# Staging all attention scores in two on-chip tiles, with partition-aligned copies in place of a trip through device memory

## The chip, the core and the metric

The kernel runs on one NeuronCore of a Trainium2 chip. Its engines work side by side and meet at semaphores: TensorE (PE; its weight loads are shown as PEld), VectorE (DVE), ScalarE (ACT), GpSimd (POOL) and SyncE (SP), whose queue issues nearly all DMAs. On-chip memory (SBUF) and the matmul accumulators (PSUM) both have 128 partitions; device memory (DRAM) is reached by DMA alone. The metric is device time in microseconds of one execution, median of several.

## What is computed

Attention with "talking heads" (a 12 by 12 mix of the heads ahead of the softmax and another behind it), followed by two dense layers of the form in, activation, out:

```python
# attention: batch 2, heads 12, positions 448, head size 64
scores = scale * q @ k.T                       # per head
scores = einsum("bhij,hg->bgij", scores, w_pre)
attn   = exp(scores - max) / (sum + 1e-9)      # over j
attn   = einsum("bgij,gh->bhij", attn, w_post)
x      = (attn @ v) as 896 rows of 768
# layer 1: h = x @ w_in (768 to 2048); g = h * clip(h + 3, 0, 6) / 6;  x = g @ w_out
# layer 2: h = x @ w_in2; g = P(h) / (Q(h) + 1e-6);                    out = g @ w_out2
```

The weights and data are float32 in value; the weights of the dense layers arrive as 64-bit words and are turned into float32 on the chip.

## The kernel before, in words

**Chunks and pairs.** The 448 query rows of a batch are cut into four chunks of 120, 120, 120 and 88 rows, eight chunks in all. A chunk is worked in groups of 10 query rows, two groups being a pair: six pairs in a chunk of 120, five in one of 88, 46 in all. The main loop has one step for each pair m, from 0 to 45.

**A step.** `premix(m)` (L265) multiplies the scores of the pair by the head-mixing weights, into two PSUM tiles M of 448 columns. The rows of a group, 10 positions times 12 heads, lie in partitions. DVE takes the row maxima (L272), ACT the exponentials (L274), `norm` gets the reciprocals (L281, L282) and POOL the scaled weights `wr` (L284). Two steps later `postmix` (L308) mixes the heads again into PSUM tile A, and `at_evac` (L316, ACT) copies it to `at`. In between, by fixed tables of step numbers, stand `scores` for a later chunk (L244: two head pairs, four matmul tiles, copied out by DVE at L249, two in the same step and two "held" for the next) and `av_unit` (L331: the product with v of an earlier chunk, X, evacuated by ACT at L343 and DVE at L344 into the high and low parts `XH` and `XL` of the layers' input).

**How scores get from "query row in partition" to "position and head in partition".** Copying out of PSUM leaves a tile with one query row per partition. `premix` needs a group's 120 (position, head) rows in partitions.
- Chunks 0 and 1 are staged whole in `stage` and `stage1`. `spread_pair` (L226) then copies a pair straight inside SBUF, as two DMAs of 210 KB (10 source partitions, 120 target partitions), to partitions 0 to 119. There `premix` multiplies with all 120 rows at once, with weights `wp0` that hold zeros for the other half.
- Chunks 2 to 7 are staged two heads at a time in a ring of four. `put_heads` (L216) sends each piece to a tile of device memory that has 60 rows and 4 zero rows per half group, and `get_pair` (L231) fetches a pair three steps ahead. There `premix` multiplies two sets of 60 rows, at partitions 0 and 64.

`stage1` occupies the memory that later becomes `XL`.

**What sets the order.** Up to L668 the order on every engine is the order of the program text; each engine works through its own queue in that order. DMAs go out on SP's queue in program order, with eight semaphores in turn, so that a ninth waits for the first. `SCORES`, `VALUES`, `LQ`, `LV` and `LK` say in which steps scores, v products and loads of q, v and k stand. The first weights of layer 1 are loaded from step 32 (`LOADS`) and converted by ACT (L399), DVE (L401, L403, L407) and POOL (L423, L424) from step 35 (`PIECES`). `FILL` puts parts of the first products of layer 1 (L351 to L353, `h`) into steps 39, 41 and 42. Behind the loop stand the last two `postmix`, the rest of those products and the last chunk's v products.

Of the kernel before, what the change touches and what calls it, by code (L numbers as in the profile page):

```python
# [48 lines left out]
def fused_kernel(  # L49
# [101 lines left out]
    nc.scalar.dma_start(out=wrep0, in_=w_pre[None, :, :].to_broadcast([GR, H, H]))  # L151
    zeros = front.tile([2 * MG * (64 - HP), S], F32, name="zeros")

    def put_pads(t):
        nc.sync.dma_start(out=t.rearrange("g (a p) s -> (g a) p s", a=2)[:, HP:], in_=zeros)

    def load_w(i):
        for a in range(0, 128, 64):
            nc.sync.dma_start(out=wrep[a : a + HP, i, :], in_=(w_pre, w_post)[i][None, :, :].to_broadcast([HR, H, H]))

    load_w(1)
# [762 lines left out]
```

## Time and profile before

| | us |
|---|---|
| median of 3 runs | 675.83 (673.94 to 678.23) |
| the profiled execution | 675.95 |
| its span, first to last instruction | 674.0 |
| first `premix` starts | 14.73 |
| last step's `premix` starts | 195.03 |
| first product of layer 1 over the second token part starts | 211.93 |

Nearly all of the kernel before 212 us is attention, all of it after that the two dense layers. A span is read from its engine's rows: start, duration, engine, line, operation, and in square brackets the idle time of the engine just before it with what ended it. "x8" merges eight instructions of one kind. A float32 matmul appears as two instructions.

### The profile page before, as it was taken

Reading aid. Unit: us, or ns where it says so; the run is one execution under the profiler, and the core shown is the slowest. Engines: PE = TensorE matmul, PEld = TensorE weight load, DVE = VectorE, ACT = ScalarE, POOL = GpSimd, SP = SyncE. Lnnn points to the kernel's source line nnn. Section 1 sums busy time; section 2 is a strip of 40 time slices with the busy share of each in tenths; the row PEclk is TensorE's granted clock in tenths of the full one; section 3 lists DMA queues with packets and bytes.
Section 4 is the critical chain, followed back from the end, with each engine's and each line's share of the span. In section 5 each row is a group of like instructions: output and inputs, shape, how many; then the busy total and the mean of one; then the engine's idle time right before and its main releaser. Section 6 shows DMA issues by size and latency. Waiting matters only on the chain.

```text
span 674.0 us, 16112 instructions
## 1 busy us (share of the span) xinstructions
PE 653.7 (97%) x6682; PEld 540.4 (80%) x6682; DVE 513.2 (76%) x879; ACT 379.0 (56%) x682; POOL 33.9 (5%) x76
## 2 busy tenths in 40 slices
PE   8998999898899999999999999999999999999997
PEld 3455556555668888988888888889999999999997
DVE  5756667676564999999866565279998999989991
ACT  4655666665664555555423323158575766779851
POOL 1110101011421000000000000000000000000000
PEclk9998999998999999999999999999999999999999
DMA  6778878897643567666542323437657665746512
GB/s 231 244 222 292 302 237 275 264 317 241 201 126 98 164 209 220 200 212 197 176 158 88 125 80 117 187 120 248 223 189 253 200 245 180 245 163 222 192 54 94
DMA packets 77503, 131.61 MB, mean 195 GB/s; under 512 B 6662, under 2 KB 57958, under 8 KB 77430
## 3 DMA queue, kind: packets, MB, share of 16 engines
q1 hardware_dynamic: 77012, 130.20, 58.8%
q8 instruction: 53, 0.87, 0.5%
q10 hardware_dynamic: 418, 0.37, 0.2%
q14 instruction: 20, 0.16, 0.1%
HBM read 90.99 MB, written 34.41 MB: 186 GB/s over the span
## 4 chain that ended last, share of the span: by engine, by line
PE 89%; DMA 3%; issue 2%; DVE 2%; ACT 2%; SPq 1%; POOL 1%; ACTq 0%; POOLq 0%; DVEq 0%
PE h L351 11%; PE h L352 11%; PE h L353 11%; PE A L308 7%; PE y L353 6%; PE y L351 6%; PE acc L351 6%; PE acc L352 6%; PE acc L353 6%; PE y L352 6%; PE M L265 6%; PE sc L244 5%; PE X L331 5%; SPq L226 1%; DMA keys<-in_k_dram 1%
## 5 line engine op out<-in xcount | busy, mean ns | idle before, releaser
L352 PE MATMUL h<-xl,wh 128*128 128x512 f32 (+1 forms) x384 | 140.1, 365 | 1.1 <-issue 1.1
L351 PE MATMUL h<-xh,wh 128*128 128x512 f32 (+1 forms) x384 | 140.6, 366 | 0.4 <-DVE g L516 0.4
L353 PE MATMUL h<-xh,wl 128*128 128x512 f32 (+1 forms) x384 | 139.1, 362 | 0.0
L272 DVE TENSOR_REDUCE st<-M 128x1 f32<-128x448 f32 x92 | 54.1, 620 | 41.8 <-PE M L265 41.0
L274 ACT ACTIVATE e<-M,st 128x448 f32<-128x448 f32 x92 | 57.6, 631 | 40.5 <-DVE st L272 40.5
L351 PEld LDWEIGHTS h<-xh,wh 128*128 128x128 f32 x384 | 72.1, 188 | 8.9 <-issue 0.8
L352 PEld LDWEIGHTS h<-xl,wh 128*128 128x128 f32 x384 | 72.2, 188 | 8.1 <-issue 1.4
L353 PEld LDWEIGHTS h<-xh,wl 128*128 128x128 f32 x384 | 72.1, 188 | 8.1
L426 ACT ACTIVATE wh<-wf 128x768 fp32r<-128x768 f32 (+1 forms) x52 | 42.6, 819 | 63.1 <-PE y L352 50.7
L427 DVE TENSOR_TENSOR wl<-wf,wh 128x768 fp32r<-128x768 f32 (+1 forms) x52 | 48.0, 924 | 36.1 <-ACT wh L426 36.1
L399 ACT ACTIVATE wf<-wraw 128x768 f32<-128x768 f32 (+1 forms) x56 | 49.5, 885 | 41.1 <-DVE wl L427 39.9
L353 PE MATMUL y<-gh,wl 128*128 128x384 f32 x192 | 70.6, 368 | 0.0
L351 PE MATMUL y<-gh,wh 128*128 128x384 f32 x192 | 70.5, 367 | 0.0
L352 PE MATMUL y<-gl,wh 128*128 128x384 f32 x192 | 69.9, 364 | 0.0
L308 PEld LDWEIGHTS A<-wr,e 60*56 60x56 f32 x2944 | 45.2, 130 | 26.7 <-issue 21.9
L316 ACT COPY at<-A 120x960 f32<-120x960 f32 x46 | 45.0, 979 | 33.2 <-PE A L308 33.0
L308 PE MATMUL A<-wr,e 60*56 60x60 f32 x2944 | 52.1, 219 | 6.6 <-issue 4.8
L403 DVE SCALAR_TENSOR_TENSOR wf<-wraw,icst,wf 128x768 int32<-128x768 int32 (+1 forms) x56 | 55.3, 988 | 1.0
L265 PE MATMUL M<-full,wp 60*64 60x448 f32 (+1 forms) x368 | 55.5, 557 | 0.3 <-ACT e L274 0.3
L407 DVE SCALAR_TENSOR_TENSOR wf<-wraw,icst,wf 128x768 int32<-128x768 int32 (+1 forms) x56 | 55.2, 986 | 0.8
L331 PEld LDWEIGHTS X<-at,vraw 120*64 120x64 f32 x768 | 37.3, 137 | 18.2 <-issue 12.5
L244 PE MATMUL sc<-keys,qraw 64*120 64x448 f32 (+1 forms) x192 | 44.3, 569 | 4.0 <-DVE xl L344 1.9
(98 smaller groups left out, 1141.8 us busy)
## 6 DMA issues: line engine op xcount, KB each, us to landing
wraw<-in_moe_w_out_dram SPq DMA_DIRECT2D x28, 768.0 KB
wraw<-in_moe_w_in_dram SPq DMA_DIRECT2D x22, 768.0 KB
full<-scores SPq DMA_DIRECT2D x34, 448.0 KB
scores<-stg SPq DMA_DIRECT2D x24, 420.0 KB
wpre<-in_moe_w_in_dram SPq DMA_DIRECT2D x10, 768.0 KB
w2h<-wh SPq DMA_DIRECT2D x16, 384.0 KB
w2l<-wl SPq DMA_DIRECT2D x16, 384.0 KB
ws<-w2h SPq DMA_DIRECT2D x16, 384.0 KB
```

The source lines that it names most:

```text
L244: nc.tensor.matmul(sc[i][:n, :S], lhsT=qraw[C][o, hp, :n], rhs=keys[b][o, hp], start=True, stop=True)
L265: nc.tensor.matmul(mt[a][64 * c : 64 * c + 64, :S], lhsT=wp[o] if C >= DIRECT else wp0[:, a], rhs=src[o if C >= DIRECT else slice(0, GR * ...
L272: nc.vector.tensor_reduce(out=st[:, a : a + 1], in_=mt[a][:, :S], op=ALU.max, axis=AX.X, negate=True)
L274: nc.scalar.activation(out=e[:, a], in_=mt[a][:, :S], func=AF.Exp, bias=st[:, a : a + 1], accum_out=st[:, 2 + a : 3 + a])
L308: nc.tensor.matmul(av[64 * c : 64 * c + JH, r, jc, :, a * HR : a * HR + HR], lhsT=e[o, a, j : j + JH], rhs=wr[o, a], start=True, stop=True,)
L331: nc.tensor.matmul(X[hh % 2 * D : hh % 2 * D + D, hh % 4 // 2, :n], lhsT=vs[:, jc, :], rhs=at[C][:, jc, hh, :n], start=(jc == 0), stop=(jc ...
L351: nc.tensor.matmul(o, lhsT=wh, rhs=mh, start=first, stop=False)
L352: nc.tensor.matmul(o, lhsT=wh, rhs=ml, start=False, stop=False)
L353: nc.tensor.matmul(o, lhsT=wl, rhs=mh, start=False, stop=last)
L399: nc.scalar.activation(out=w, in_=hw.bitcast(F32), func=AF.Copy, scale=2.0**-112)
L403: nc.vector.scalar_tensor_tensor(out=wi, in0=hw, scalar=icst[:, 0:1], in1=wi, op0=ALU.bitwise_and, op1=ALU.bitwise_or)
L407: nc.vector.scalar_tensor_tensor(out=wi, in0=lw, scalar=icst[:, 1:2], in1=wi, op0=ALU.logical_shift_right, op1=ALU.bitwise_or)
```

## The change

All eight chunks are staged whole, in two tiles used in turn (`stages[C % 2]`). `spread_pair` copies every pair inside SBUF, into partitions 4 to 123 of a ring of five pairs (`first`); partitions 0 to 3 are zeroed once. A group's rows then lie in partitions 4 to 63 and 64 to 123, and `premix` of every pair multiplies two sets (64 and 60 rows). The device-memory tiles, `put_heads`, `get_pair`, their zero rows and `wp0` go; `XL` gets memory of its own. The pair for step m + 4 is copied in step m. A chunk's scores stand nine, seven and five steps ahead of its first pair. The weights' pool opens in step 37, where the front pool is freed; each weight tile is loaded in three DMAs. `FILL` goes, and the products that it placed stand behind the loop.

```diff
+LOW = 64 - HP
 NCH = 4
 MG = CH // GR
 NP = H // 2
-DIRECT = 2
-LEAD = 3
+RING = 5
...
-    scd = {}
-    sct = [dram.tile([MG, 128, S], F32, name=f"scores{i}") for i in range(3)]
-
...
-    wrep = front.tile([128, 2, H], F32, name="wrep")
-    mask0 = front.tile([GR * H, GR], F32, name="mask0")
-    wrep0 = front.tile([GR * H, H], F32, name="wrep0")
+    wrep = front.tile([128, H], F32, name="wrep")
+    mask0 = front.tile([128, 2, HR], F32, name="mask0")
+    wrep0 = front.tile([128, H], F32, name="wrep0")
+    first = att.tile([128, RING, 2, S], F32, tag="first", bufs=1, name="first")
+    stages = [att.tile([CH, H, S], F32, tag=f"stage{i}", bufs=1, name=f"stage{i}") for i in range(2)]
...
     XH = xp.tile([128, KD, NT], F32R, name="xh")
-    place = xp.tile([128, KD, NT], F32, tag="xl", name="stage1")
-    stage1 = place.rearrange("p c t -> p (c t)").rearrange("p (h s) -> p h s", s=S)[:CH]
-
+    XL = xp.tile([128, KD, NT], F32R, name="xl")
...
+    nc.vector.memset(first[:LOW, :2], 0.0)
...
+    nc.gpsimd.memset(wp, 0.0)
+    nc.gpsimd.memset(first[:LOW, 2:], 0.0)
...
-    def put_heads(C, hp, st):
-        n = chunks[C][3]
-        rows = scd[C][:n].rearrange("g (a p) s -> (g a) p s", a=2)[:, :HP]
-        nc.sync.dma_start(
-            out=rows.rearrange("x (i h) s -> x i (h s)", h=H)[:, :, 2 * hp * S : (2 * hp + 2) * S],
-            in_=st[: n * GR].rearrange("p h s -> p (h s)"),
-        )
-
     def spread_pair(m):
         C, g0 = pairs[m]
-        full[m] = spread.tile([128, 2, S], F32, tag="first", bufs=NP, name=f"full{m}")
-        rows = (stage, stage1)[C].rearrange("p h s -> p (h s)").rearrange("(r g) x -> g r x", g=MG)
+        full[m] = first[:, m % RING]
+        G = chunks[C][3]
+        rows = stages[C % 2][: G * GR].rearrange("p h s -> p (h s)").rearrange("(r g) x -> g r x", g=G)
         for c in range(2):
-            nc.sync.dma_start(out=full[m][: GR * H, c, :], in_=rows[g0 + c])
-
-    def get_pair(m):
-        C, g = pairs[m]
-        full[m] = att.tile([128, 2, S], F32, tag="full", bufs=LEAD, name=f"full{m}")
-        nc.sync.dma_start(out=full[m], in_=scd[C][g : g + 2].rearrange("g p s -> p g s"))
-
-
-    def scores(C, hp, tag="sc", st=None):
+            nc.sync.dma_start(out=full[m][LOW : LOW + GR * H, c, :], in_=rows[g0 + c])
+
+    def scores(C, hp, tag="sc"):
         n = chunks[C][3] * GR
         b = chunks[C][0]
-        if hp == 0:
-            scd[C] = sct[C % 3]
         sc = [ps.tile([128, 512], F32, tag=tag, bufs=BUFS[tag], name=f"sc{C}_{2 * hp + i}") for i in range(2)]
-        if st is None:
-            st = front.tile([CH, 2, S], F32, tag="raw", bufs=4, name=f"stg{C}_{hp}")
+        st = stages[C % 2][:, 2 * hp : 2 * hp + 2]
         for i in range(2):
             o = slice(i * D, i * D + D)
...
-        def take(i, copy):
-            copy(out=st[:n, i], in_=sc[i][:n, :S])
-            if i and C > 1:
-                put_heads(C, hp, st)
-
-        return [lambda copy: take(0, copy), lambda copy: take(1, copy)]
+        return [lambda copy, i=i: copy(out=st[:n, i], in_=sc[i][:n, :S]) for i in range(2)]
...
-                o = slice(64 * a, 64 * a + HP)
+                o = slice(64 * a, 64 + a * HP)
                 nc.tensor.matmul(
-                    mt[a][64 * c : 64 * c + 64, :S], lhsT=wp[o] if C >= DIRECT else wp0[:, a],
-                    rhs=src[o if C >= DIRECT else slice(0, GR * H), c, :], start=True, stop=True,
+                    mt[a][64 * c : 64 * c + 64, :S], lhsT=wp[o],
+                    rhs=src[o, c, :], start=True, stop=True,
...
+    def load_third(u, i):
+        u = units[u]
+        if i == 0:
+            raws[u] = (pools["late"].tile([128, KD * 256], I32, tag="wraw", bufs=2, name="wraw"), KD)
+        n = KD // THIRDS
+        o = raws[u][0].rearrange("p (a b) -> p a b", b=256)[:, i * n : i * n + n]
+        nc.sync.dma_start(out=o, in_=w1i[:, i * n : i * n + n, u[1] * 256 : u[1] * 256 + 256])
...
     for m in range(3):
         spread_pair(m)
     load_q(2)
-    for m in range(3, NP):
+    for m in range(3, RING):
         spread_pair(m)
-    for a in range(2):
-        mix_in(wp0[:, a, :HP].rearrange("p (i g) -> p i g", g=H), mask0[:, a * HR : a * HR + HR], wrep0)
+    mix_in(wp[:, :HP].rearrange("p (i g) -> p i g", g=H), mask0[:, 0], wrep0)
...
     NC = len(chunks)
-    SCORES = list(range(1, 36, 2))
-    VALUES = list(range(8, 38, 2)) + [37, 38, 40, 43, 44, 45]
+    SCORES = [begin[C] - i for C in range(2, NC) for i in (9, 7, 5)]
+    VALUES = [8, 10, 12, 15, 17, 19, 21, 23, 25, 27, 29, 31, 33, 35, 37, 38, 40, 42, 43, 44, 45]
     SC = per_step([(0, (1, hp)) for hp in range(FIRST, NP)] + list(zip(
         sorted(2 * SCORES), [(C, hp) for C in range(2, NC) for hp in range(NP)])))
     XS = per_step(list(zip(
         sorted(2 * VALUES), [(C, i) for C in range(NC - 1) for i in range(NP)])))
-    LQ = {3: 3, 10: 4, 15: 5, 21: 6, 27: 7}
-    LV, LK = {4: 2, 6: 3, 8: 4, 9: 5}, {8: 0, 10: 1, 11: 2, 12: 3, 14: 4, 15: 5}
-    FREE = max(SC) + 2
-    LATE, LOADS = 20, {32: 0, 34: 1, 38: 2, 41: 3}
-    PIECES = dict(zip(range(35, 46), (1, 2, 2, 1, 2, 1, 1, 2, 1, 1, 1)))
-    FILL = {39: (0, 3), 41: (0, 3), 42: (1, 3)}
-    early = {}
-
+    LQ = {2: 3, 8: 4, 14: 5, 19: 6, 25: 7}
+    LV, LK = {3: 2, 5: 3, 6: 4, 7: 5}, {9: 0, 10: 1, 11: 2, 12: 3, 13: 4, 15: 5}
+    LV1 = 28
+    FREE = max(SC) + 1
+    PIECES = dict(zip(range(38, 46), (1, 2, 2, 2, 1, 2, 2, 1)))
+    LOADS = {37: ((0, 0), (0, 1), (0, 2)), 38: ((1, 0), (1, 1)), 39: ((1, 2),)}
+    LOADS.update({40: ((2, 0),), 41: ((2, 1), (2, 2)), 43: ((3, 0), (3, 1)), 44: ((3, 2),)})
...
-        if 1 <= m <= NP:
-            spread_pair(m + NP - 1)
...
-        if first[DIRECT] <= m + LEAD < len(pairs):
-            get_pair(m + LEAD)
...
+        if 1 <= m <= len(pairs) - RING:
+            spread_pair(m + RING - 1)
...
         if m == FREE:
             front.release()
-        if m == LATE:
-            spread.release()
             pools["late"] = tc.alloc_tile_pool(name="late", bufs=1, side="right", reuse_waits="tile")
...
-        if m in LOADS:
-            load_units(LOADS[m])
-        if m in FILL:
-            f, n = FILL[m]
-            if f not in early:
-                early[f] = gemm1(f, 0, ps.tile([128, 512], F32, tag="sc", bufs=BUFS["sc"], name=f"h1_{f}_0"))
-            for _ in range(n):
-                next(early[f])
+        for x in LOADS.get(m, ()):
+            load_third(*x)
     m = len(pairs)
...
-    run(early[1])
+    run(gemm1(0, 0, ps.tile([128, 512], F32, tag="sc", bufs=BUFS["sc"], name="h1_0_0")))
     postmix(m - 2)
     at_evac(m - 2, acopy)
-    h120 = gemm1(2, 0, ps.tile([128, 512], F32, tag="sc", bufs=BUFS["sc"], name="h1_2_0"))
+    h110 = gemm1(1, 0, ps.tile([128, 512], F32, tag="sc", bufs=BUFS["sc"], name="h1_1_0"))
     for _ in range(3):
-        next(h120)
+        next(h110)
     postmix(m - 1)
     at_evac(m - 1, acopy)
     pieces(1)
-    run(h120)
+    run(h110)
     for i in range(NP):
         tail_x(2 * i + 1, "sc" if i < 2 else "M")
+    run(gemm1(2, 0, ps.tile([128, 512], F32, tag="sc", bufs=BUFS["sc"], name="h1_2_0")))
...
+    ucur[0] = 4
     load_units(4)
...
         rows = _np.array([[c[1] + row_of(c, g) + i for g in range(c[3])] for i in range(GR)])
-        rows = q[c[0], :, (rows if C < DIRECT else rows.T).ravel()].reshape(c[3] * GR, NP, 2, D)
+        rows = q[c[0], :, rows.ravel()].reshape(c[3] * GR, NP, 2, D)
```

**SP's queue, around the first pair of chunk 2, before** (`full` is a pair's tile, `stg` two heads of staged scores, `scores_110` and `scores_112` tiles in device memory):

```order
L231 DMA full_795<-scores_112 128x2x448
L135 DMA vraw_5_797<-in_v_dram 120x512
L216 DMA scores_110<-stg_2_801 20x5x896
L231 DMA full_861<-scores_112 128x2x448
L125 DMA qraw_863<-in_q_dram 128x720
L131 DMA keys_721<-in_k_dram 128x448
```

**SP's queue, the same place now** (`stage_128` and `stage_127` are the two staging tiles, `first` the ring):

```order
L130 DMA vraw_5_607<-in_v_dram 120x512
L207 DMA first<-stage_128 120x1x448 x2
L120 DMA qraw_670<-in_q_dram 128x720
L207 DMA first<-stage_127 120x1x448 x2
L126 DMA keys_745<-in_k_dram 128x448
```

A step's one put and one get have become two copies inside SBUF, of half the size each.

**ACT, steps 35 to 36 before** (`e` exponentials, `at` copies, `wf` the first conversion of weight tile 0):

```order
L274 ACTIVATE e_2614,st_2613<-M_0_2607,st_2613 128x448
L274 ACTIVATE e_2614,st_2613<-M_1_2608,st_2613 128x448
L316 COPY at_2350<-A 120x2x48x10
L399 ACTIVATE wf<-wraw 128x768
L274 ACTIVATE e_2680,st_2679<-M_0_2673,st_2679 128x448
```

**ACT now, step 38 and the start of 39:**

```order
L241 ACTIVATE e_2707,st_2706<-M_0_2700,st_2706 128x448
L241 ACTIVATE e_2707,st_2706<-M_1_2701,st_2706 128x448
L310 ACTIVATE xh<-X_1_2712 128x2x120
L283 COPY at_2648<-A 120x2x48x10
L376 ACTIVATE wf<-wraw 128x768
L241 ACTIVATE e_2782,st_2781<-M_0_2775,st_2781 128x448
```

The first conversion stood three steps behind the step of its load, and now stands one step behind it, ahead of step 39's exponentials.

**PE, step 39 before, to the start of step 40** (`M` is premix, `A` postmix, `h_0_0` the first product of layer 1):

```order
L265 MATMUL M_0_2900<-full_2685,wp 64x448 x2
L265 MATMUL M_1_2901<-full_2685,wp 64x448 x2
L308 MATMUL A<-wr_2816,e_2755 56x12x5 x32
L351 MATMUL h_0_0_2953<-xh,wh 128x384
L352 MATMUL h_0_0_2953<-xl,wh 128x384
L353 MATMUL h_0_0_2953<-xh,wl 128x384
...
L265 MATMUL M_0_2963<-full_2760,wp 64x448 x2
```

**PE, step 39 and 40 now:**

```order
L232 MATMUL M_0_2775<-first,wp 64x448 x2
L232 MATMUL M_1_2776<-first,wp 64x448 x2
L275 MATMUL A<-wr_2689,e_2626 56x12x5 x32
L232 MATMUL M_0_2829<-first,wp 64x448 x2
L232 MATMUL M_1_2830<-first,wp 64x448 x2
```

Step 39 has lost its nine products of layer 1; all of `h_0_0` now follows the last step's `postmix`.

## Rows read from the trace of the kernel before

**Rows 1.** The page, part 1: busy time, share of the span, instructions

```profile
PE 653.7 (97%) x6682; PEld 540.4 (80%) x6682; DVE 513.2 (76%) x879; ACT 379.0 (56%) x682; POOL 33.9 (5%) x76
```

**Rows 2.** Windows: stretch, length, busy of PE, PEld, DVE, ACT, POOL, clock, DMA, GB/s

```profile
14.73:64.43 49.70, 47.42 (x858) 24.17 (x860) 32.14 (x75) 26.16 (x60) 4.91 (x13) 0.97 0.78 252
64.43:195.03 130.60, 119.59 (x3091) 78.12 (x3081) 86.66 (x207) 83.75 (x186) 22.14 (x39) 0.99 0.79 253
172.00:200.00 28.00, 25.48 (x643) 18.60 (x631) 17.44 (x38) 16.65 (x37) 9.02 (x10) 1.00 0.44 138
```

**Rows 3.** Timeline of PE, step 5, premix over 120 rows

```profile
31.48 1.72 PE L265 MATMUL M<-full,wp 120*64 120x448 f32 x8
33.14 1.77 PE L244 MATMUL sc<-keys,qraw 64*120 64x448 f32 x8
```

**Rows 4.** Timeline of PE, steps 21 to 23, premix over twice 60 rows

```profile
99.32 0.94 PE L265 MATMUL M<-full,wp 60*64 60x448 f32 x8
100.19 1.77 PE L244 MATMUL sc<-keys,qraw 64*120 64x448 f32 x8
...
102.77 0.94 PE L265 MATMUL M<-full,wp 60*64 60x448 f32 x8
...
106.31 0.94 PE L265 MATMUL M<-full,wp 60*64 60x448 f32 x8
```

**Rows 5.** Timeline of DVE, one short step

```profile
22.88 1.35 DVE L272 TENSOR_REDUCE st<-M 128x1 f32<-128x448 f32 x2 [0.30 <-PE M L265]
24.15 1.15 DVE L249 COPY stg<-sc 120x448 f32<-120x448 f32 x2
...
25.53 1.35 DVE L272 TENSOR_REDUCE st<-M 128x1 f32<-128x448 f32 x2
```

**Rows 6.** Timelines of SP, DVE and PE around step 9

```profile
44.58 2.69 SPq L226 DMA_DIRECT2D full<-stage  x2
51.98 0.41 DVE L344 TENSOR_TENSOR xl<-X,xh 128x240 fp32r<-128x240 f32 x1 [5.44 <-DMA scores<-stg]
52.45 1.29 PE L244 MATMUL sc<-keys,qraw 64*100 64x448 f32 x2 [1.95 <-DVE xl L344]
53.67 1.86 PE L308 MATMUL A<-wr,e 60*56 60x60 f32 x64
55.46 2.18 PE L265 MATMUL M<-full,wp 120*64 120x448 f32 x8
```

**Rows 7.** Timeline of SP: one row is so many DMAs issued together

```profile
10.93 4.98 SPq L226 DMA_DIRECT2D full<-stage  x6
```

**Rows 8.** What PE waited for, 64.43 to 195.03: total, times, longest

```profile
PE A L308 <- issue: 4.8, 5, 2.1
PE X L331 <- issue: 2.0, 3, 0.9
PE h L352 <- issue: 1.1, 1, 1.1
PE sc L244 <- DVE st L272: 1.1, 1, 1.1
```

**Rows 9.** Chain of waits: one 768 KB weight load, start and duration

```profile
212.08 4.68 DMA wpre<-in_moe_w_in_dram
```

**Rows 10.** Timeline of DVE: pieces of a weight tile's conversion

```profile
182.94 0.54 DVE L401 TENSOR_SCALAR wf<-wf 128x768 int32<-128x768 int32 x1
186.89 1.00 DVE L403 SCALAR_TENSOR_TENSOR wf<-wraw,icst,wf 128x768 int32<-128x768 int32 x1
```

**Rows 11.** Timeline of PE behind the loop

```profile
202.60 1.07 PE L308 MATMUL A<-wr,e 60*56 60x60 f32 x64 [0.78 <-ACT at L316]
203.60 0.45 PE L351 MATMUL h<-xh,wh 128*128 128x384 f32 x1
...
205.37 1.06 PE L308 MATMUL A<-wr,e 60*56 60x60 f32 x64
...
211.93 0.50 PE L351 MATMUL h<-xh,wh 128*128 128x512 f32 x1
```

More of the change, by code (lines that the diff above doesn't have):

```diff
@@ L123, in load_q @@
         ns = chunks[C][3] * GR
-        t = front.tile([128, NP, CH], F32, tag="qraw", bufs=3, name=f"qraw{C}")
+        t = front.tile([128, NP, CH], F32, tag="qraw", bufs=2, name=f"qraw{C}")
         eng.dma_start(out=t[:, :, :ns], in_=q[C, :, :, :ns])
@@ L150, in fused_kernel @@
     load_q(1)
[L151 to L161, printed above, removed]
-    nc.gpsimd.memset(mask0, 1.0)
-    nc.gpsimd.affine_select(out=mask0, in_=mask0, pattern=[[-H, GR]], compare_op=ALU.is_ge,
-                            fill=0.0, base=0, channel_multiplier=1)
-    nc.gpsimd.affine_select(out=mask0, in_=mask0, pattern=[[H, GR]], compare_op=ALU.is_ge,
-                            fill=0.0, base=H - 1, channel_multiplier=-1)
-    nc.gpsimd.memset(wp0, 0.0)
-    nc.gpsimd.memset(zeros, 0.0)
-    put_pads(sct[2])
+    nc.scalar.dma_start(out=wrep0[LOW : LOW + GR * H], in_=w_pre[None, :, :].to_broadcast([GR, H, H]))
+    for a in range(0, 128, 64):
+        nc.sync.dma_start(out=wrep[a : a + HP], in_=w_post[None, :, :].to_broadcast([HR, H, H]))
+    nc.gpsimd.memset(mask0, 1.0)
+    nc.gpsimd.affine_select(out=mask0, in_=mask0, pattern=[[-HP, 2], [-H, HR]], compare_op=ALU.is_ge,
+                            fill=0.0, base=-LOW, channel_multiplier=1)
+    nc.gpsimd.affine_select(out=mask0, in_=mask0, pattern=[[HP, 2], [H, HR]], compare_op=ALU.is_ge,
+                            fill=0.0, base=H - 1 + LOW, channel_multiplier=-1)
+    nc.gpsimd.tensor_tensor(out=mask0[:, 0], in0=mask0[:, 0], in1=mask0[:, 1], op=ALU.add)
+    nc.gpsimd.memset(wp, 0.0)
+    nc.gpsimd.memset(first[:LOW, 2:], 0.0)
     for hp in range(2):
@@ L451, in advance @@
         split_units(i + 1)
-    stage = att.tile([CH, H, S], F32, tag="at", bufs=2, name="stage")
     manual = tc.manual_schedule()
@@ L460, in fused_kernel @@
     for hp in range(NP):
-        ev = scores(0, hp, "sc" if hp % 3 else "M", stage[:, 2 * hp : 2 * hp + 2])
+        ev = scores(0, hp, "sc" if hp % 3 else "M")
         ev[0](acopy)
         ev[1](vcopy)
-    def place1(hp):
-        return stage1[:, 2 * hp : 2 * hp + 2]
     for m in range(3):
@@ L521, in fused_kernel @@
     LAG = 2
-    first = [m for m, (C, g) in enumerate(pairs) if g == 0] + [len(pairs)]
+    begin = [m for m, (C, g) in enumerate(pairs) if g == 0] + [len(pairs)]
     def per_step(items):
@@ L571, in fused_kernel @@
             load_v(0, LV[m])
-        if 27 <= m < 27 + NP:
-            load_v(1, m - 27)
+        if LV1 <= m < LV1 + NP:
+            load_v(1, m - LV1)
         if m in LK:
@@ L577, in fused_kernel @@
         for C, hp in SC.get(m, ()):
-            sc += scores(C, hp, st=place1(hp) if C == 1 else None)
+            sc += scores(C, hp)
         for C, i in XS.get(m, ()):
```

19 lines of the change are left out of this document (5 added, 14 removed).

## The prediction

> **What bounds the kernel now.** I read the page first, then the windows by stage, then the timelines of PE, DVE and SP in the attention, and last what PE waited for. The page makes PE the busiest engine by far [rows 1]. That share hides two things: the attention consists of short steps with waits between them, and behind it PE is dense, with the change touching nothing there but the weights that arrive first. So I cost the stretch from the first premix (14.73) to the first product over the second token part (211.93), 197.2 us, and let the rest shift with it. The profiled execution took 675.95 for a span of 674.0, 0.12 above the median; the sum is made against it.
>
> In that stretch a step lasts as long as PE's work in it, when nothing stalls: 3.45 us from premix to premix with scores in it, 3.54 with v products [rows 4]. Steps with neither are held by a loop instead: DVE's maxima, ACT's exponentials, DVE's reciprocal, then the next maxima, 2.65 us from maximum to maximum [rows 5]. The v product and the score copies fit into that loop's gaps.
>
> **What the change removes.**
> - Premix over 120 rows takes 1.66 us to the next operation [rows 3]; over two sets of 60 rows it takes 0.87 [rows 4]. Twelve pairs change, 9.5 us. All else in premix stays; 64 rows instead of 60 stream the same 448 columns, so I take 0.87.
> - The stall of step 9. DVE's first write to `XL` waited 5.44 us for DMAs, since `XL` lies where chunk 1 was staged and the last copy out of it left SP's queue at 47.27 only. PE stood still for 1.95 us, and then ran slow: the clock of the stretch is 0.97 [rows 2], two score instructions took 1.29 instead of 0.43, postmix 1.86 instead of 1.07, premix 2.18 instead of 1.72 [rows 6]. With the gap, 4.0 us go.
> - Device-memory traffic: each of 34 pairs goes through a put and a get of over 400 KB each, and now through one copy of 420 KB. The DMA engines were 0.79 busy [rows 2].
>
> **What it adds.**
> - SP: two issues of 0.83 us each for a pair [rows 7] in place of one put and one get. Under load a pair's issues took 2.69 [rows 6]; both are below a step with its other load beside them, and a pair is copied four steps ahead, so I cost it at nothing. If that cover went, every pair would be late (a rival below). Ahead of the first premix nothing is longer: ten copies instead of twelve, and memsets on engines that stand idle there.
> - Shorter premix makes the short steps PE-idle: steps 1, 2, 4 and 6 have only 0.87 to 1.9 us of PE work and fall back to the loop's 2.65. In step 1, where no postmix stands yet, PE idles for nearly 2 us. By the row after the 1.95 us gap that costs 2.1 more at the lower clock (0.86, 0.79 and 0.46 [rows 6]). Bounds 0 and 2.1; I take 2.1, since the gap is as long.
> - Steps 13 and 14 both carry scores. The second's tiles wait for held copies; the nearest row is a wait of scores for DVE, 1.1 us [rows 8].
> - Weights. The first tile is asked for in step 37 behind two copies, and ACT converts it at the end of step 38, ahead of step 39's exponentials. 768 KB alone took 4.68 us [rows 9]. Behind DVE's last score copies (premix 0.87, maxima 1.35, copies 1.15 [rows 4, 5], 3.4 in all) and the pair's 1.7 us of issue it lands 9.8 us after step 37 starts; ACT gets to it after about 8, a step of 3.54 and the most of another. Bounds: 0, and 4 if the copies hold the load up; I take 1.8.
> - DVE's conversion pieces crowd into steps 39 to 44: 0.55 and 1.0 us apiece [rows 10] on top of the loop. Steps 39 and 41 take 2.65 + 1.55 = 4.2, steps 40 and 42 about 4, step 43 3.6, step 44 about 5, 25 in all. PE may run a premix ahead, so I take 24, against 19.5 without pieces. GpSimd's splits fit before their users.
> - The products taken out of steps 39, 41 and 42 stand behind the loop. There, 9.33 us from postmix 44 on [rows 11] stay, and two whole products (twice 18 matmuls, nine in 1.77 [rows 11]) come on top, 7.1. The wait of 0.78 for ACT goes, hidden by the first of them.
>
> **The sum.** Step 0: 0.87 + 1.70 = 2.6. Four short steps 10.6. Steps 39 to 44: 24. The other 35 at 3.5: 122.5. Tail 9.3 + 7.1 = 16.4. Together 176.1. The same count for the kernel before (premix at 1.66 in steps 0 to 11, nine products in each of steps 39, 41 and 42) is 165.0 for its steps and 11.2 for its tail, 176.2. So the count is a draw: what premix saves, short steps and DVE's pieces take. The gain must come out of the waits, 197.2 − 176.2 = 21 us before. Of these, 4.0 is step 9, 1.1 scores' wait for DVE [rows 8], 0.8 the tail; the other 15 are "issue" waits of PE (4.8 + 2.0 + 1.1 = 7.9 [rows 8]), a second slow stretch behind the longest of them, and small waits.
>
> The issue waits decide the size. They begin with the gets: there is none before 64 us, although DMA was as busy (0.78 and 0.79 [rows 2]). Two of the nine fall where DMA was down to 0.44 [rows 2], each some 5 us behind the issue of a weight load. I read them as PE's instructions held up behind other DMAs. Half the traffic goes, so I take 6.3 of the 15: half of the issue waits, a third of the rest. Bounds 0 and 15, the latter if the early steps, now denser, catch them too.
>
> The Trainium skill, "Runtime: NRT & Kernel Launch", section "Instruction fetch mechanics", says that an engine's instructions come over a DMA queue of its own in blocks of 256, and that crossing a block is mostly hidden. By that rule the 6.3 would be 0 and the time 659; the rows' 7.9 us speak against it.
>
> Waits after: 2.1 + 1.1 + 1.8 + 6.3 = 11.3. Stretch 176.1 + 11.3 = 187.4, 9.8 less than before: 675.95 − 9.8 = 666.2. Three v steps are narrower than I counted, which takes off about 1: **665 us**.
>
> **Rivals.**
> - *The fetch waits vanish* with the traffic: 665 − 6.3 = 659. For it: none in the early steps. Against it: the two at 0.44. Chance 0.18.
> - *They stay or grow*, since they go by instructions and not by traffic: 13 to 15 in place of 6.3, 672. For it: the two at 0.44. Chance 0.18.
> - *Late weights stall ACT for longer.* Tiles 0 and 1 come 2 us later than taken, each stall in front of exponentials idles PE for over 2 us and costs another 2 at the lower clock: 665 + 6 to 7 = 671. Chance 0.08.
> - *Slower: the first pair of every chunk comes late.* Nothing of a chunk can be copied before its last score is staged, which happens in the fourth step ahead of its first pair. From there: 3.4 us to DVE's last copy, 1.7 to 2.7 for SP, and landing, 4.7 for the copy whose issue ended at 47.27 and for which DVE waited until 51.98 [rows 6]. That is 10 to 11 us of four steps' 14. Landing would have to take 12 instead of 4.7; then each of six chunks loses 3.5 us, and the time is 665 + 21 = 686. The decisive point is landing above 8 us. Chance 0.06.
>
> On this last one the Trainium skill, "DMA: Bandwidth & Descriptors", section "Why a DMA increments its semaphore by 16 and not by 1", speaks against the change: the number of DMA engines is the largest up to 16 that divides the outermost sizes of both sides, so 10 for these copies (10 and 120) and 16 for a get. By the row, 210 KB in 0.83 us of issue, two copies fill 1.7 of 3.5 us even so.
>
> **Chances and range.** The forecast itself, 660 to 669, has 0.50. What can be told from no change is 1%, 669.1 and 682.6. Below 669.1: nearly all of the forecast and the first rival, 0.68. Within 1%: the second and third, 0.26. Slower: 0.06. The range 656 to 674 reaches from the first rival to the second with a few us of the unknown costs, and leaves the last out.
>
> **What would show it.** After the change: premix at 0.87 in all steps; no DVE wait for a DMA at step 9; PE idle of 0.8 to 2 us in steps 1, 2, 4 and 6, with a clock below 1 behind step 1; DVE without gaps from step 39 to 44; issue waits of PE in total near half of 7.9; the first product over the second token part near 201. It is wrong if premix waits for DMAs, if the issue waits are not halved, or if ACT's first conversion waits long.

## The result and the profile after

| | before | after |
|---|---|---|
| median of four runs, us | 675.8 (673.94 to 678.23) | 666.53 (665.61 to 669.0) |
| profiled execution, us (span) | 675.95 (674.0) | 665.91 (664.2) |
| stretch, first premix to first product over the second token part | 197.2 | 186.37 |

The ratio is 0.987, with a 95% interval of 0.982 to 0.991: 1.3% faster. On another chip, beside the variants below, the same kernel took 666.96 (664.74 to 667.68) against 677.16, ratio 0.985 (0.981 to 0.989). The forecast was 665, in 656 to 674. The span fell by 9.8 us: the stretch by 10.83, less 0.54 that the first premix started later in this execution and 0.49 behind the stretch.

| part of the stretch, us | before | after |
|---|---|---|
| steps 0 to 11 | 49.70 | 40.11 |
| steps 12 to 38 | 105.83 | 95.86 |
| steps 39 to 44 | 24.77 | 29.70 |
| step 45 | 4.96 | 4.30 |
| tail: from the first product behind the loop | 11.94 | 16.40 |

So 20.2 us were gained, and 9.4 of them went again at the loop's end and behind it, where the products from steps 39, 41 and 42 now stand.

**The early steps.** Timeline of PE in the changed kernel, steps 9 to 11 (columns: start, duration, what, tiles, shapes, number of instructions; in brackets the idle time before it and what ended it):

```profile
44.97 0.94 PE L232 MATMUL M<-first,wp 64*64 64x448 f32 x8
45.84 1.75 PE L216 MATMUL sc<-keys,qraw 64*100 64x448 f32 x8
47.52 1.06 PE L275 MATMUL A<-wr,e 60*56 60x60 f32 x64
48.40 0.94 PE L232 MATMUL M<-first,wp 64*64 64x448 f32 x8
...
51.95 0.94 PE L232 MATMUL M<-first,wp 64*64 64x448 f32 x8
```

This is where [rows 6] stood. Premix takes 0.87 to the next operation, step 9 takes 3.43 us instead of 8.36, and no engine waits for a DMA in these steps.

**The middle.** Windows of the changed kernel: stretch, its length, busy time of PE, PEld, DVE, ACT and POOL, clock, DMA share, GB/s. The first covers steps 0 to 12, one step more than the first of [rows 2]; the last is premix 39 to premix 45:

```profile
15.27:58.92 43.65, 40.35 (x952) 22.26 (x956) 31.52 (x78) 28.19 (x66) 4.64 (x12) 1.00 0.71 226
58.92:144.15 85.23, 83.97 (x2200) 51.06 (x2192) 63.59 (x160) 58.44 (x132) 9.28 (x24) 1.00 0.48 158
64.00:195.00 131.00, 122.36 (x3140) 81.02 (x3140) 90.27 (x210) 84.28 (x186) 20.59 (x38) 0.97 0.45 144
151.24:180.94 29.70, 22.80 (x577) 15.37 (x565) 16.55 (x33) 16.25 (x35) 7.91 (x10) 0.89 0.54 167
```

From 59 to 144 us PE stands still for 1.3 of 85 us. What it waited for up to 202 us (total, times, longest), beside [rows 8]:

```profile
PE M L232 <- ACT e L241: 7.8, 5, 4.0
PE A L275 <- ACT at L283: 2.2, 5, 0.5
...
PE A L275 <- issue: 0.3, 1, 0.3
```

The issue waits, in which PE waits for nothing that this view names, are down from 7.9 us to 0.3, and a new wait heads the list: premix for ACT's exponentials.

**The new loss.** Timelines of PE, ACT, DVE and SP in steps 37 to 41:

```profile
151.24 0.95 PE L232 MATMUL M<-first,wp 64*64 64x448 f32 x8
152.61 1.06 PE L275 MATMUL A<-wr,e 60*56 60x60 f32 x64 [0.41 <-ACT at L283]
157.67 2.38 PE L232 MATMUL M<-first,wp 64*64 64x448 f32 x8 [4.00 <-ACT e L241]
159.98 3.47 PE L298 MATMUL X<-at,vraw 120*64 120x120 f32 x32
...
151.48 0.98 ACT L283 COPY at<-A 120x960 f32<-120x960 f32 x1 [0.40 <-PE A L275]
156.11 0.89 ACT L376 ACTIVATE wf<-wraw 128x768 f32<-128x768 f32 x1 [3.65 <-DMA wraw<-in_moe_w_in_dram]
156.90 0.62 ACT L241 ACTIVATE e<-M,st 128x448 f32<-128x448 f32 x1
...
146.29 1.15 DVE L220 COPY stage<-sc 100x448 f32<-100x448 f32 x2
...
133.27 15.87 SPq L207 DMA_DIRECT2D first<-stage  x8
149.24 3.90 SPq L346 DMA_DIRECT2D wraw<-in_moe_w_in_dram  x3
```

Read from below. The load of weight tile 0 leaves SP from 149.24 on, 5.1 us after step 37 began (144.15), behind two copies that wait for DVE's last score copies (these end at 147.44, and the row of eight copies hides that the last two are issued from 147.50 on). It is there at 156.11, and ACT, which got to the conversion at 152.46, stood 3.65 us in front of it. The exponentials of step 39 are queued behind on ACT, so PE idles for 4.00 us, and then premix and v product run at the lower of the two levels, 1.2 GHz (the granted clock is 0.50 from 157.67 to 163.40): 2.38 and 3.47 instead of 0.94 and 1.86. Together 7.05 us.

**The end.** The first product behind the loop starts at 185.24, and the tail takes 16.40 us from there:

```profile
185.24 0.44 PE L318 MATMUL h<-xh,wh 128*128 128x384 f32 x1
...
201.64 0.39 PE L318 MATMUL h<-xh,wh 128*128 128x512 f32 x1
```

### The profile page after: what moved, and what is told of

Read it like the earlier page. It is cut to its first block, busy times and chain, and to the rows that moved or that the text cites. A ratio compares the mean times of both kernels' runs of the same rounds, so it can differ in the third digit from the quotient of the medians.

```text
span 664.2 us, 16127 instructions
## 1 busy us (share of the span) xinstructions
PE 645.7 (97%) x6681; PEld 537.2 (81%) x6682; DVE 514.2 (77%) x880; ACT 377.6 (57%) x682; POOL 34.2 (5%) x73
## 4 chain that ended last, share of the span: by engine, by line
PE 89%; DVE 4%; ACT 3%; DMA 2%; issue 1%; POOL 0%; SPq 0%; POOLq 0%; DVEq 0%; ACTq 0%
PE h L318 11%; PE h L319 11%; PE h L320 11%; PE y L318 6%; PE y L320 6%; PE acc L318 6%; PE acc L320 6%; PE acc L319 6%; PE y L319 6%; PE sc L216 6%; PE A L275 5%; PE X L298 5%; PE M L232 5%; ACT e L241 1%; DMA first<-stage 1%
## 5 line engine op out<-in xcount | busy, mean ns | idle before, releaser
L275 PEld LDWEIGHTS A<-wr,e 60*56 60x56 f32 x2944 | 43.6, 127 | 21.7 <-issue 18.7
L232 PE MATMUL M<-first,wp 60*64 60x448 f32 (+1 forms) x368 | 50.0, 554 | 8.1 <-ACT e L241 7.8
L220 DVE COPY stage<-sc 120x448 f32<-120x448 f32 (+1 forms) x85 | 49.1, 616 | 7.2 <-PE sc L216 4.5
L275 PE MATMUL A<-wr,e 60*56 60x60 f32 x2944 | 49.7, 216 | 2.5 <-ACT at L283 2.2
L298 PEld LDWEIGHTS X<-at,vraw 120*64 120x64 f32 x768 | 38.3, 140 | 16.4 <-DVE st L249 7.0
```

What stands on the lines that cost most here:

```text
L220: return [lambda copy, i=i: copy(out=st[:n, i], in_=sc[i][:n, :S]) for i in range(2)]
L232: nc.tensor.matmul(mt[a][64 * c : 64 * c + 64, :S], lhsT=wp[o], rhs=src[o, c, :], start=True, stop=True,)
L275: nc.tensor.matmul(av[64 * c : 64 * c + JH, r, jc, :, a * HR : a * HR + HR], lhsT=e[o, a, j : j + JH], rhs=wr[o, a], start=True, stop=True,)
L298: nc.tensor.matmul(X[hh % 2 * D : hh % 2 * D + D, hh % 4 // 2, :n], lhsT=vs[:, jc, :], rhs=at[C][:, jc, hh, :n], start=(jc == 0), stop=(jc ...
```

## The experiments

Three questions: what did the late tile cost, where did the issue waits go, and what did the shorter premix bring? Times are medians; ratios are to the kernel before on the same chip. Of the changed kernel's variants only four are clear of it by their intervals (743.82 and 703.64 us above it, 657.88 and 657.06 below). What the others show is read from their traces, one execution each.

### Tile 0 asked for ahead of the copies

```diff
+        if m == FREE:            # step 37, now ahead of spread_pair
+            front.release(); ...
+            for x in LOADS[m]:
+                load_third(*x)
         if 1 <= m <= len(pairs) - RING:
             spread_pair(m + RING - 1)
```

> The three thirds of weight tile 0 are asked for at the start of step 37, ahead of that step's two copies, instead of behind them; nothing else changes. Theory (the load is late because it stands behind copies that wait for DVE's last score copies): it is issued near 145.5 instead of 149.2, lands near 152, ACT does not wait at 152.5, and the 4.00 us gap with its 3.05 us at the lower clock goes: 659 to 661. Rival (the load itself is slow, 6.9 us instead of 4.7, since it shares the DMA engines with the copies): it lands at 153 to 155, ACT waits 1 to 2.5 us, half of the gap stays: 662 to 664.

662.44 us (661.44 to 664.15), ratio 0.977 (0.970 to 0.984). Timelines of SP, ACT and PE:

```profile
142.66 1.69 SPq L346 DMA_DIRECT2D wraw<-in_moe_w_in_dram  x3
146.72 4.38 SPq L207 DMA_DIRECT2D first<-stage  x4
...
151.61 0.90 ACT L376 ACTIVATE wf<-wraw 128x768 f32<-128x768 f32 x1
...
153.19 1.59 PE L232 MATMUL M<-first,wp 64*64 64x448 f32 x8 [0.26 <-ACT e L241]
...
160.37 0.89 ACT L376 ACTIVATE wf<-wraw 128x768 f32<-128x768 f32 x1 [1.60 <-issue]
161.92 1.76 PE L232 MATMUL M<-first,wp 64*64 64x448 f32 x8 [1.95 <-ACT e L241]
```

The load now leaves SP 0.75 us ahead of premix 37 (143.41), ACT does not wait for tile 0, and the 4.00 us gap is 0.26. So the cause of that gap is the place in SP's queue. But premix 39 to premix 45 still takes 25.83 us instead of 29.70: of 7.05 us, 3.9 are gained, and the rest comes back two steps later, where ACT now waits 1.60 us in front of tile 1's conversion. The row says "issue", but by the trace the last third of tile 1 landed at 160.30, 0.07 us before ACT began. The time is the rival's, 662 to 664, but not for its reason.

### The conversion one step later

```diff
-    PIECES = dict(zip(range(38, 46), (1, 2, 2, 2, 1, 2, 2, 1)))
+    PIECES = dict(zip(range(39, 46), (1, 2, 2, 2, 2, 2, 2)))
...
-    LOADS.update({40: ((2, 0),), 41: ((2, 1), (2, 2)), 43: ((3, 0), (3, 1)), 44: ((3, 2),)})
+    LOADS.update({41: ((2, 0), (2, 1)), 42: ((2, 2),), 43: ((3, 0), (3, 1)), 44: ((3, 2),)})
```

> ACT's first weight conversion stands one step later (end of step 39 instead of 38), the other pieces and the loads of weight tiles 2 and 3 follow it; nothing else changes. Theory (the late weight tile holds ACT in front of step 39's exponentials, which idles PE for 4.00 us and then slows premix and v product by another 3.05): ACT finds the tile at 156.1 after reaching the conversion near 155.2, waits under 1 us, PE's gap behind step 39 falls to 1.5 or less, premix 40 is back at 0.94, and the profiled time is 5 to 7 us below 665.9: 659 to 661. Rival (PE in steps 39 to 45 is held by DVE's crowded pieces anyway, the wait merely stands in for them): the gaps come back later in steps 41 to 45 and the time is 664 to 666. Second rival (the tile lands later still because its load runs beside other copies): ACT waits over 2 us again, 663 or more.

665.42 us (663.17 to 665.93), ratio 0.980 (0.974 to 0.985), no gain that can be told from the change. The first wait fell below 1 us as the theory said, but the gaps came back later, as the first rival had it. Timeline of ACT:

```profile
156.26 0.94 ACT L376 ACTIVATE wf<-wraw 128x768 f32<-128x768 f32 x1 [0.93 <-DMA first<-stage]
...
165.81 0.91 ACT L376 ACTIVATE wf<-wraw 128x768 f32<-128x768 f32 x1 [2.13 <-issue]
...
188.17 0.89 ACT L376 ACTIVATE wf<-wraw 128x768 f32<-128x768 f32 x1 [4.65 <-DMA wraw<-in_moe_w_in_dram]
```

Tile 1's conversion (165.81; by the trace its last third landed at 165.67) and the one behind the loop (188.17) stand and wait instead. The latter is of a later weight tile, whose load left SP only at 183.40.

### Both tiles first, and DVE's pieces moved

```diff
-    LOADS = {37: ((0, 0), (0, 1), (0, 2)), 38: ((1, 0), (1, 1)), 39: ((1, 2),)}
+    LOADS = {37: ((0, 0), (0, 1), (0, 2), (1, 0), (1, 1), (1, 2))}     # ahead of the copies
```

> As the kernel with tile 0 asked for ahead of step 37's copies, and weight tile 1's three thirds right behind it, instead of behind the copies of steps 38 and 39. Theory (what is left of the loss is again a conversion that waits for its load: there ACT waited 1.60 us for tile 1 at 160.4): that wait goes with the slow clock behind it, 2 to 3 us below the 662.4 median of the kernel with tile 0 first: near 660. Rival (DVE's pieces hold steps 39 to 45 by themselves): less than 1 us, 662. Rival (six thirds ahead of the copies make the copies of pairs 41 and 42 late): premix waits for DMA first<-stage, slower.

662.82 us (662.63 to 668.73), ratio 0.983 (0.977 to 0.989). ACT waits for no tile in the loop any more, and nothing that can be told was gained by it: the first rival. Then, on top of it:

```diff
+        pieces(BEFORE.get(m, 0))     # DVE's pieces of steps 39 to 44
         norm(m)
...
         pieces(PIECES.get(m, 0))     # only ACT's and GpSimd's are left here
...
-    PIECES = dict(zip(range(38, 46), (1, 2, 2, 2, 1, 2, 2, 1)))
+    PIECES = {38: 1, 40: 1, 42: 1, 45: 1}
+    BEFORE = {39: 2, 40: 1, 41: 2, 42: 1, 43: 2, 44: 1}
...
+    LOADS.update({40: ((2, 0), (2, 1), (2, 2)), 42: ((3, 0), (3, 1), (3, 2))})   # earlier too
```

> As the kernel with tiles 0 and 1 asked for first, and in steps 39 to 44 DVE's conversion pieces stand between the maxima and the normalisation, where DVE otherwise waits 0.94 us for ACT's exponentials, not behind it; tile 2 is loaded at the end of step 40, tile 3 at the end of step 42. Theory (in these steps the loop maxima, exponentials, normalisation, pieces, next maxima sets the pace): steps 39 to 44 take 20 to 21 us from premix 39 to premix 45 instead of 25.8 with tile 0 first alone, and the time is 655 to 658. Rival (the waits of ACT for loads hold them, not DVE's order): as with both tiles first, within 1 us, 660.

657.88 us (655.81 to 661.04), ratio 0.974 (0.969 to 0.979). Timelines of DVE and PE with both tiles early, then of DVE and ACT with the pieces moved as well:

```profile
160.87 1.15 DVE L239 TENSOR_REDUCE st<-M 128x1 f32<-128x448 f32 x2
162.95 0.83 DVE L248 TENSOR_SCALAR st<-st 128x2 f32<-128x2 f32 x1 [0.94 <-ACT e L241]
...
163.90 0.54 DVE L378 TENSOR_SCALAR wf<-wf 128x768 int32<-128x768 int32 x1
164.48 1.02 DVE L380 SCALAR_TENSOR_TENSOR wf<-wraw,icst,wf 128x768 int32<-128x768 int32 x1
165.42 1.14 DVE L239 TENSOR_REDUCE st<-M 128x1 f32<-128x448 f32 x2
...
173.43 1.81 DVE L378 TENSOR_SCALAR wf<-wf 128x768 int32<-128x768 int32 x1 [1.54 <-ACT wf L376]
...
176.64 1.85 PE L232 MATMUL M<-first,wp 64*64 64x448 f32 x8 [1.59 <-ACT e L241]
178.42 3.22 PE L298 MATMUL X<-at,vraw 120*64 120x120 f32 x32
```

```profile
163.67 1.15 DVE L239 TENSOR_REDUCE st<-M 128x1 f32<-128x448 f32 x2
164.74 1.01 DVE L384 SCALAR_TENSOR_TENSOR wf<-wraw,icst,wf 128x768 int32<-128x768 int32 x1
165.76 0.17 DVE L248 TENSOR_SCALAR st<-st 128x2 f32<-128x2 f32 x1
...
167.25 0.93 ACT L376 ACTIVATE wf<-wraw 128x768 f32<-128x768 f32 x1
```

DVE's queue is worked off in order. Behind the maxima it stands 0.94 us until ACT has the exponentials, and the pieces come after that, on the loop's path. Ahead of the normalisation they fill that wait. Premix 39 to premix 45 takes 21.28 us, against 24.61 with both tiles early alone.

The edit does a second thing, though. ACT's conversion of tile 2 stood in step 43, right ahead of the DVE piece that needs it; now it stands at the end of step 42 (167.25), and tiles 2 and 3 are asked for earlier. With both tiles early alone that DVE piece waited 1.54 us for ACT, ahead of the next maxima; PE then stood still for 1.59 us, and the v product behind it took 3.22 instead of 1.86. Of the 3.33 us between the two kernels' rows, 1.78 lie in step 44, behind that wait, and 1.55 in steps 41 to 43. So how much of the gain is DVE's order and how much the earlier conversion is not shown: no run has the one without the other.

### The pieces alone

The same edit to the changed kernel, the earlier tiles 2 and 3 included, with tiles 0 and 1 asked for as there.

> Only the pieces between maxima and normalisation (and with them the loads of tiles 2 and 3); tiles 0 and 1 are asked for as in the changed kernel, behind the copies. Theory (two separate losses, each by itself: the late tile 4.00 us of gap and 3.05 at the lower clock, DVE's order 4 to 5): ACT still waits 3.65 us for tile 0 and PE stands still for 4, and the time is 661 to 664. Rival (the late tile is what counts, the order only pays once it is on time): 665 to 667.

664.07 us (661.73 to 666.37), ratio 0.981 (0.977 to 0.986), against 666.96 for the change on the same chip. ACT still waits 3.55 us and PE 3.9. The edit gains 2.9 us with the tile late, which is not clear of noise (the change's runs reach from 664.74 to 667.68), and 4.9 with it on time. That fits two losses that are largely separate; it does not prove it.

### Issue waits: traffic put back, and taken away

```diff
+    def traffic(m):              # in steps 1 to 36, behind the pair's copies
+        nc.sync.dma_start(out=junk_d[m % 3], in_=junk)        # first run only
+        nc.sync.dma_start(out=t, in_=k[0, :, 0:4:3])          # both runs
```

> In steps 1 to 36 each pair's two copies are followed by a dummy write of 420 KB to device memory and a dummy read of 448 KB from it, on the same queue, which nothing waits for; the output is not touched. This puts back the device-memory traffic that the change took out, without the waits on it. Theory (PE's issue waits are instructions held up behind other DMAs, so they went with the traffic): DMA share between 58.9 and 110 goes from 0.44 to about 0.8, issue waits come back with 4 to 8 us up to 200 against 0.3, with slow stretches behind the longest; 670 to 676. Rival (they went with something else, such as the order of the instructions or the get's place ahead of premix): issue waits stay below 1 us and the time is 665 to 668, with at most small waits for later copies. If the copies come late under the load, premix waits for DMA first<-stage, which would be told apart by its releaser.

743.82 us, ratio 1.096 (1.090 to 1.102): not by the theory. What DVE waited for there, 64 to 195 us (lines are moved by the edit; L228 is the score copy):

```profile
DVE stage L228 <- DMA first<-stage: 32.0, 3, 14.7
...
DVE stage L228 <- DMA junk_d<-junk: 9.6, 1, 9.6
```

The copies out of a staging tile were so late that the scores that overwrite it waited up to 14.7 us. Issue waits came to 1.8 us at a DMA share of 0.83, with PE standing still a quarter of the time for that other reason, so this run leaves them open. The next halves the dummy traffic:

> The changed kernel with one dummy read of 448 KB from device memory behind each pair's two copies in steps 1 to 36, which nothing uses: half of the traffic of the last such run, so that the copies should still come in time. Theory (issue waits follow DMA traffic): DMA share between 58.9 and 110 near 0.65 to 0.7, issue waits of 2 to 5 us up to 200 against 0.3, 668 to 672. Rival (they do not follow traffic): below 1 us, 665 to 668. If the copies are late again, DVE's score copies wait for DMA first<-stage, and the run tells of that alone.

703.64 us, ratio 1.041 (1.036 to 1.046), far above the theory's 668 to 672, at a DMA share of 0.84 where I had expected 0.65 to 0.7. DVE's copies wait here too, but for less. And the kernel before, with its reads taken out:

```diff
     def get_pair(m):
-        full[m] = att.tile([128, 2, S], F32, tag="full", bufs=LEAD, name=f"full{m}")
-        nc.sync.dma_start(out=full[m], in_=scd[C][g : g + 2].rearrange("g p s -> p g s"))
+        full[m] = fulls[m % LEAD]
```

> The kernel before without the reads of scores back from device memory: from pair 12 on premix reads zeros from three fixed tiles, so the outputs of those chunks are not the reference's; all writes to device memory and all else stay. Theory (PE's issue waits follow DMA traffic): DMA share 64 to 195 falls from 0.79 to about 0.45, the issue waits from 7.9 to under 2 us, and with the slow stretch behind the longest the time falls by 6 to 12 us to 664 to 670. Rival (they belong to PE's instructions as they stand in this kernel): 5 to 8 us of issue waits stay and the time is 674 to 677. Second rival (they belong to premix's wait for the read itself): they vanish at any DMA share.

667.91 us (665.7 to 672.9), ratio 0.987 (0.982 to 0.993): taking out the reads alone is worth as much as the whole change. The trace is of the longest execution, 672.9, in which the stall of step 9 [rows 6] was 4.0 us long instead of 1.95. Waits of PE and windows from 64 to 195 us, first of the change with dummy reads (L279 is postmix, L302 the v product), then of the kernel before without reads (L307 is postmix):

```profile
PE A L279 <- issue: 11.1, 5, 3.1
...
PE X L302 <- issue: 1.5, 1, 1.5
...
64.00:195.00 131.00, 107.44 (x2560) 67.10 (x2556) 72.31 (x179) 66.75 (x152) 10.43 (x27) 0.91 0.84 225
```

```profile
PE A L307 <- issue: 2.6, 2, 2.3
...
64.00:195.00 131.00, 126.20 (x3208) 80.78 (x3199) 91.98 (x218) 87.69 (x195) 22.29 (x40) 0.99 0.50 144
```

Issue waits in 131 us by DMA share: 0.3 us at 0.45, 2.6 at 0.50 (the theory had under 2), 7.9 at 0.79 [rows 2, 8], 12.6 at 0.84. They come back with the reads in the changed kernel, where no engine uses what is read, so they are not premix's wait for a read; and they fall when the reads are taken out of the kernel before. But the share is not all there is to it: besides the 1.8 us at 0.83, there is no issue wait at all from 15 to 64 us, neither in the kernel before at a share of 0.78 nor with the dummy reads at 0.87.

What PE waits for can be read from the traces. The page of the profile lists a DMA queue of its own for instructions; here it is for the kernel before (packets, MB, share):

```profile
q8 instruction: 53, 0.87, 0.5%
```

Each packet is a block of 16 KB, and the trace has its time. Every one of the 25 issue waits of PE from 14 to 205 us, in all fourteen traces, ends 1.2 to 1.7 us after such a block has landed. About 25 blocks land in 131 us, so a time picked at random would do so about once in ten. Some of them:

| kernel | issue wait, us | it ends at | a block landed at | us between |
|---|---|---|---|---|
| before | 2.10 | 152.20 | 150.63 | 1.57 |
| before | 1.10 | 174.70 | 173.19 | 1.51 |
| the change | 0.34 | 113.27 | 111.79 | 1.48 |
| with dummy reads | 3.13 | 122.16 | 120.75 | 1.41 |
| with dummy reads | 2.54 | 172.23 | 170.80 | 1.43 |
| before, without reads | 2.29 | 136.69 | 135.27 | 1.42 |

So PE waits for its next block of instructions. The transfers themselves hardly differ: their median time over the whole execution is 1.00 us in the kernel before, 1.07 in the change and 1.09 with dummy reads. In the longest wait PE had stood still for 0.56 us when the block's transfer began, at 119.59. Whether the blocks were asked for late or stood behind other DMAs, no row tells.

### Premix over all rows again, and a smaller ring

```diff
-                o = slice(64 * a, 64 + a * HP)
+                o = slice(0, 124) if m < 12 else slice(64 * a, 64 + a * HP)
```

> Premix of the first 12 pairs contracts over 124 rows again, as one set; all else stays. Its weights are those of the new layout, so the mixed scores of these pairs are not the reference's: only the time is read. Theory (the short steps 1, 2, 4 and 6 are held by the loop over DVE and ACT, so the halved premix pays only in the eight other steps, by 0.79 each, and a little of it stands beside the loop): 6 us slower than the profiled 665.9, 670 to 673. Rival (it pays in all twelve): 9.5 us, 675. Rival (steps are held by the loop everywhere in this stretch): below 2 us, 666 to 668.

671.23 us (669.16 to 674.26), ratio 0.989 (0.983 to 0.996), against 0.985 (0.981 to 0.989) for the change: as the theory's 670 to 673 had it, but not clear of noise. By the traces, steps 0 to 13 take 51.30 us (14.28 to 65.58) instead of 47.09 (15.27 to 62.36), 4.2 us more. So the shorter premix pays 0.7 to 0.9 us in steps 0, 9, 10 and 11, and 0.34 or less in the others: a step with scores behind a short step is held by the loop as well, which I had not counted. The theory's eight paying steps are four.

```diff
-RING = 5
+RING = 4
```

> Ring of four pairs instead of five, so each pair is copied three steps ahead of its premix instead of four. Theory (a copy needs 1.7 us of issue and about 4.7 us to land, so three steps of 3.5 are enough for premix; but the last copies out of a staging tile now end a step later, closer to the scores that overwrite it): no premix waits for a copy; DVE's score copies wait for DMA first<-stage where a chunk has five pairs (step 14, 3 to 6 us) and up to 2 us in the other chunks; 670 to 678. Rival (the slack is larger, the landing under 3 us): within 2 us of the change, 665 to 669. Rival (first pairs late, as in the slower forecast): premix waits for DMA first<-stage in each chunk, 675 or more.

664.55 us (661.9 to 666.13), ratio 0.981 (0.977 to 0.986): not slower, so the theory's total fell. Timelines of DVE, PE and SP:

```profile
28.45 1.16 DVE L220 COPY stage<-sc 120x448 f32<-120x448 f32 x2 [2.93 <-DMA first<-stage]
...
31.27 2.37 PE L232 MATMUL M<-first,wp 64*64 64x448 f32 x8 [1.56 <-ACT e L241]
33.57 3.34 PE L216 MATMUL sc<-keys,qraw 64*120 64x448 f32 x8
...
147.71 2.27 SPq L346 DMA_DIRECT2D wraw<-in_moe_w_in_dram  x3
```

The longest wait for the staging tile is 2.93 us, in step 3 and not in step 14, and no premix waits for a copy even at three steps. The change has a wait of 2.00 us at the same place, and PE hardly notices it (0.57 us); with 0.9 more, PE stands still for 1.56 and the rows behind are slow. Steps 0 to 13 take 52.07 us instead of 47.09. It was paid back at the other end: in step 37 the pair being copied is now one whose scores were long staged, so tile 0 is asked for 0.67 us ahead of premix 37 (148.38), and ACT does not wait for it: the place in SP's queue once more.

### The change with both losses taken away

```diff
+        if m in (FREE, FREE + 1):     # tile 0 first in step 37, tile 1 first in step 38
+            for x in LOADS[m]:
+                load_third(*x)
```

and DVE's pieces in front of the normalisation.

> Pieces between maxima and normalisation as in the kernel with 657.9; tile 0 asked for first in step 37 and tile 1 first in step 38, instead of both in step 37. There, PE had 1.3 us of issue waits while both tiles were loading (step 38 took 4.78 us instead of 3.55). Theory (issue waits follow the load on the DMA engines, and one tile at a time loads them less): these go and steps 38 and 39 are back at 3.55, 1 us less: 655 to 657. Rival (tile 1 now comes late for ACT in step 40): a wait of ACT for wraw of 1 to 2 us and 658 to 660.

> The changed kernel once more, on the same chip as these, to set them against: 665 to 669 by every theory.

657.06 us (656.39 to 658.13), ratio 0.971 (0.967 to 0.975), against 666.96 and 0.985 for the change on the same chip: 9.9 us less than the change and 20 less than before. The issue waits are gone from the list, but ACT now waits 1.76 us for tile 2, so the two versions of the load order are about even. Window from 150 to 190 us, the change and then this kernel:

```profile
150.00:190.00 40.00, 33.09 (x822) 23.85 (x817) 23.06 (x46) 22.36 (x51) 11.31 (x14) 0.91 0.49 150
```

```profile
150.00:190.00 40.00, 37.75 (x976) 29.17 (x968) 24.93 (x52) 25.62 (x54) 11.00 (x14) 1.00 0.55 167
```

PE is busy for 4.7 us more of the same 40, at a granted clock of 1.00 instead of 0.91.

## Why the prediction was right

The total was, and three of its terms were not; they cancelled: short steps 1.9 us less than forecast, steps 39 to 44 3.9 more, the other steps 2.1 less. That the sum comes out so near is luck.

| part of the stretch, us | predicted, waits included | measured |
|---|---|---|
| step 0 | 2.6 | 2.62 |
| steps 1, 2, 4, 6 | 10.6 + 2.1 | 10.83 |
| steps 39 to 44 | 24 + 1.8 | 29.70 |
| the other 35 steps | 122.5 + 1.1 + 6.3 | 126.82 |
| tail | 16.4 | 16.40 |
| sum | 187.4, less 1 for three narrower v steps | 186.37 |

- **Step 9.** Forecast 4.0 of stall and 0.8 of premix, 8.36 became 3.43. Right.
- **Short steps.** Right at 2.65 apiece, 2.71 on average. The 2.1 us at a lower clock behind step 1 did not come: the granted clock of the early steps is 1.00, and the scores behind take 1.77. PE's waits there were 1.3 us at most.
- **Weights.** The step that failed. "Bounds: 0, and 4 if the copies hold the load up; I take 1.8." Issue was forecast right (149.2), but it took 6.87 us from the first issue until ACT had the tile instead of 4.68, and its three issues alone took 3.90. ACT waited 3.65, just inside the bounds, and PE paid 7.05, outside them: I priced ACT's wait and left out the slow rows behind PE's gap, though [rows 6] show just such a gap and my third rival had that price for a stall. Of my own signs of being wrong, this one appeared: ACT's first conversion waited long.
- **DVE in steps 39 to 44.** I expected it without gaps. It had 0.94 us or more in each, in front of the normalisation, and 1.54 in front of a piece that waited for ACT's conversion of tile 2; the edit that removed both was worth 4.9 us.
- **The other 35 steps.** 129.9 forecast less that 1, 126.82 measured. Issue waits nearly went, but steps 3, 5, 7 and 8 took 3.95 to 4.10 us instead of 3.5, 2.25 in all, for which I had no term.
- **Issue waits.** I halved them; they vanished, which is the first rival's mechanism. That they go with other DMAs was read rightly, as the two runs with reads put in and taken away show; the size was not. That PE's own instructions are what is held up is shown by the blocks that land 1.2 to 1.7 us before each wait ends. The Trainium skill, "Runtime: NRT & Kernel Launch", section "Instruction fetch mechanics", has the crossing mostly hidden: that agrees with the change, one wait of 0.3 us in 131 us and 25 blocks, and less with the dummy reads, where six of 21 blocks cost 12.6 us.
- **The slower rival.** Its late copies did not come, not even with three steps of lead; landing was never the limit by itself. The runs with dummy traffic show the limit elsewhere: at the staging tiles, whose next scores wait for the copies out of them.

So two rivals came true at once, the first (659) and, with one stall at its price, the third (671), and the total lies between them.

## What to carry to other kernels

When a wait is priced, the slow rows behind such a gap on the same engine belong to the price, as in [rows 6] here. A load that is asked for behind a transfer which itself waits on an engine is late by that engine's time: order a queue by when things can start, not by step. Where an engine's queue has a wait in every round, put its optional work in front of that wait, and have its inputs ready a step earlier; here the two together took 4.9 us off. And an issue wait need not stay a guess: look on the instruction queue for the block that lands just before it ends.

## What the runs showed of the hardware

- PE's issue waits are waits for 16 KB blocks of its instructions: all 25 end 1.2 to 1.7 us after a block has landed. Their total went from 0.3 us in 131 at a DMA share of 0.45 to 12.6 at 0.84; I had expected something like proportion. The share alone does not set them: none from 15 to 64 us at 0.87, and 1.8 at 0.83 in another run.
- One 448 KB read for each pair raised the DMA share from 0.45 to 0.84 (GB/s from 144 to 225) and made the kernel 37 us longer than the change: the share rose 1.9-fold for 1.6 times the bytes per second.
- Three issues of 256 KB on SP took 3.90 us behind the pair's copies, and 1.69 to 2.27 when tile 0 stood ahead of them.
